# Accumulating the cosine layers' seven-product sums in PSUM, and writing the scales' diagonal one step ahead

## The chip, the cores and the metric

The kernel runs on one core of one Trainium2 chip. The metric is device time in microseconds; the kernel before takes 1402.75 us (median of three runs, 1401.98 to 1403.76). The engines are named as in the profile: PE is the matrix engine (TensorE), PEld its weight loads, DVE is VectorE, ACT is ScalarE, POOL is GpSimd and SP is SyncE, which issues transfers. Each engine carries out its instructions in the order in which they were recorded, and waits where an operand is not there yet.

## The reference

Three stages follow each other. Attention has 2 batches, 8 heads, 768 positions and a head size of 64, with four sink columns and a window of 128. Its output, 1536 tokens by 512, goes to a mixture of 8 ReLU experts whose gate is normalised eight times by rows and columns. The last stage multiplies by the cosine:

```python
for e in range(E):                       # 8 experts, 512 -> 1024 -> 512
    h = np.maximum(x @ w1[e], 0.0)
    out += P[:, e:e+1] * (h @ w2[e])
...
h = x @ w_in                             # 512 -> 2048
g = h * np.cos(h)
return g @ w_out                         # 2048 -> 512
```

All is float32, so the kernel splits each float32 operand, scaled by a power of two, into a high and a low float16 half, and multiplies three times (high by high, high by low, low by high).

## The kernel before

The last stage is cut into two halves of 1024 hidden columns, and so has the shape of two more experts: `e` runs from 0 to 9, where 0 to 7 are ReLU experts and 8 and 9 are cosine experts. Each runs for batch `b` = 0 and then 1 (768 tokens each). The four passes with `e` of 8 and 9 are called the cosine layers C0 to C3 here.

A layer begins with its first multiplication, x by w1. It is done with seven products in place of eight (Winograd's form of Strassen's scheme): tokens are cut into two halves of 384, hidden columns into 4 pairs of blocks, `j` = 0 to 3, of 128 columns. For each `j` the products 0 to 6 are six matmuls of 128x384 each, and four blocks come out: `j` (low) and `NJ + j` (high), each for both halves of the tokens. A product with its surroundings is a step; `tick()` at its end records what other work is due there (loads, splits of the next weights, parts of the cosine). Such work is put on the list with `put(t0, every, steps)`, and `flush()` first runs what is in the list `late`.

In ReLU layers (`g1`, L925) products 0, 4, 3, 6 of a chain pile up in one bank of PSUM ("A"), 5 and 2 in another ("B"), 1 in a third ("C"). Between them ACT copies the sum out (L930), because each partial sum is needed by itself, and DVE adds two of them (L934). In cosine layers (`g1_sums`, L968) each product has a bank of its own, from a ring of five, and the sums are made by DVE: 7 adds per chain (L989) after one copy by ACT (L997).

A block h then goes through `act_cos` (L881): ACT converts it to whole turns (L887), DVE reduces it (L890), ACT takes Sin and Square (L895, L896), DVE multiplies by h (L899), and POOL writes the high half (L901) and the low half (L903) into HH. These parts are recorded one to three steps after each other.

The second multiplication (`g2_mm`, L1021) takes three matmuls of 128x512 per tile of 128 tokens and block of 128 columns: an item. There are 6 tiles and 8 blocks in a layer, so 48 items. In cosine layers the items of three tiles are put beside the products of the first multiplication (the list `fill`): when a chain `j` begins, the items of chain `j - 1` are appended, and one item is recorded after each product (none in the last chain, where six are kept back, `KEEP = 6`). The other three tiles follow whole.

A scale (`scales`, L122) needs the largest of 128 partial maxima, one in each partition. DVE cuts it to a power of two and multiplies the unit matrix by it (L144, the diagonal), PE multiplies a matrix of ones with the diagonal (L145), so that every partition holds all 128 values, and one step later DVE takes the maximum (L149) and its reciprocal. Diagonal and product are recorded in the same step. With several scales at once (attention's values) all diagonals share one tile, so each waits for the product before it.

Of the kernel before, what the change touches and what calls it, by code (L numbers as in the profile page):

```python
# [40 lines left out]
def kernel(  # L41
# [14 lines left out]
    nc = tc.nc  # L56
# [62 lines left out]
    diag = res.tile([128, 128], BF16, name="diag")  # L119
    top_bank = ["l"]  # L120

    def scales(parts, n, clamp, keep, tag, then, squares=False):  # L122
# [36 lines left out]
        late.append(rest)  # L159
# [140 lines left out]
    def attention():  # L300
# [411 lines left out]
        put(10, 1, p0[7:9])  # L712
        put(11, 0.5, p0[9:-1:2])
# [83 lines left out]
    def experts(before):  # L797
# [83 lines left out]
        def act_cos(src, ft, half, sc):  # L881
# [26 lines left out]
        KEEP = 6  # L908
        pend = []

        def settle():
            if pend:
                pend.pop()()
# [11 lines left out]
        def g1(b, j0, chain, act):  # L925
# [42 lines left out]
        def g1_sums(b, j, act, fill, keep):  # L968
            q = {}

            def prod(o, use):

                ps = ring["g1"].next()[:, 0:HT]
                n = 0
                for kk in range(2):
                    for wi, xi in ((0, 0), (0, 1), (1, 0)):
                        nc.tensor.matmul(  # L977
                            ps, W1O[:, j, wi, o, kk, :], XO[b][:, kk, o, xi, :],
                            start=(n == 0), stop=(n == 5))
                        n += 1  # L980
                if len(fill) > keep:
                    fill.popleft()()
                settle()
                pend.append(lambda: use(ps))
                tick()

            def add(tag, x, y):
                t = ring[tag].next()
                nc.vector.tensor_tensor(out=t, in0=x, in1=y, op=ALU.add)  # L989
                return t  # L990

            def out(x, y, ft, half):
                act(add("c", x, y), ft, half)

            def use0(ps):
                q["p0"] = ring["t"].next()
                nc.scalar.activation(out=q["p0"], in_=ps, func=AF.Copy)  # L997

            def use4(ps):
                q["u"] = add("t", ps, q["p0"])  # L1000

            def use5(ps):
                q["u5"] = add("t", ps, q["u"])

            def use3(ps):
                out(ps, q["u5"], NJ + j, 1)
                q["v"] = add("t", ps, q["u"])

            prod(0, use0)
            prod(4, use4)  # L1010
            prod(1, lambda ps: out(ps, q["p0"], j, 0))
            prod(5, use5)
            prod(2, lambda ps: out(ps, q["u5"], NJ + j, 0))
            prod(3, use3)
            prod(6, lambda ps: out(ps, q["v"], j, 1))


        orders = ([0, NJ, 1, NJ + 1, NJ + 2, NJ + 3, 2, 3], [f for j in range(NJ) for f in (j, NJ + j)])
# [13 lines left out]
        def layers(e, b, act, so):  # L1032
# [4 lines left out]
            top_bank[0] = "l" if e < E else "g1"  # L1037
            if e < E:
                for j0 in range(0, NJ, 2):
                    g1(b, j0, CHAIN if e or b else ONE, act)  # L1040
            else:

                for j in range(NJ):
                    if j == 1:
                        ps = {t: ring["g2"].next() for t in range(U3)}
                    for f in (j - 1, NJ + j - 1) if j else ():
                        for t in ps:
                            fill.append(lambda t=t, f=f: g2_mm(e, t, ps[t], [f], False))
                    g1_sums(b, j, act, fill, KEEP if j == NJ - 1 else 0)
# [14 lines left out]
            if e >= E:  # L1064
                for t in ps:
                    fill.append(lambda t=t: g2_mm(e, t, ps[t], order[-2:-1]))
                m = len(fill)
                for k in range(m):
                    fill.popleft()()
                    for _ in range(U3 * (NJ - 1) * k // m, U3 * (NJ - 1) * (k + 1) // m):  # L1070
                        tick()
                late = order[-1:]
            for t in tiles if e < E else range(NT):
                if t in ps:
                    g2_mm(e, t, ps[t], late)
# [72 lines left out]
        for e in range(E + 2):  # L1148
# [3 lines left out]
            if e == E:  # L1152
                banks(g1=(2, 3, 6, 0, 1))
                ring.update(t=Ring(TMP[:, n] for n in range(4)), c=Ring(TMP[:, n] for n in range(4, 9)))
# [88 lines left out]
```

## Time and profile before

| | |
|---|---|
| median of 3 runs | 1402.75 us |
| profiled execution | 1399.94 us, its span 1398.2 us |
| PE busy | 1289.7 us (92%) |
| DVE, ACT, POOL busy | 896.0, 694.1, 641.2 us |
| mean granted clock of PE | 0.964 |
| C0, C1, C2, C3 | 76.08, 61.43, 64.44, 62.21 us |

Times in the trace count from the first instruction. A timeline row gives start, duration, engine, line, operation, tiles, shapes and, in brackets, how long the engine had stood idle and what ended it. The source lines are those of the kernel above; the row of a helper names the helper's line. The last matmul's end of a row is modelled, and a row overlaps with the next.

### The profile page before, as it was taken

Reading aid. Unit: us, or ns where it says so; the run is one execution under the profiler, and the core shown is the slowest. Engines: PE = TensorE matmul, PEld = TensorE weight load, DVE = VectorE, ACT = ScalarE, POOL = GpSimd, SP = SyncE. Lnnn points to the kernel's source line nnn. Section 1 sums busy time; section 2 is a strip of 40 time slices with the busy share of each in tenths; the row PEclk is TensorE's granted clock in tenths of the full one; section 3 lists DMA queues with packets and bytes.
Section 4 is the critical chain, followed back from the end, with each engine's and each line's share of the span. In section 5 each row is a group of like instructions: output and inputs, shape, how many; then the busy total and the mean of one; then the engine's idle time right before and its main releaser. Section 6 shows DMA issues by size and latency. Waiting matters only on the chain.

```text
span 1398.2 us, 19777 instructions
## 1 busy us (share of the span) xinstructions
PE 1289.7 (92%) x7299; PEld 683.2 (49%) x7299; DVE 896.0 (64%) x1853; ACT 694.1 (50%) x1374; POOL 641.2 (46%) x782
## 2 busy tenths in 40 slices
PE   5657899999999999999999999999999987998998
PEld 4533455454554545455454555545455443444444
DVE  8996762865556653855655575484565689678664
ACT  5654664462635346164443616436263647566443
POOL 4555463521524264163336427234442657276534
PEclk7767899999999999999999999999999999999999
DMA  9997663011112310501331050141112232200001
GB/s 233 164 166 175 119 138 101 1 61 61 61 61 73 124 59 7 191 1 60 92 106 61 30 166 1 60 133 64 61 38 81 47 93 54 74 1 0 31 16 45
DMA packets 140689, 108.78 MB, mean 78 GB/s; under 512 B 100144, under 2 KB 115504, under 8 KB 140592
## 3 DMA queue, kind: packets, MB, share of 16 engines
q1 hardware_dynamic: 126512, 77.22, 21.6%
q0 software_dynamic: 7168, 25.17, 5.9%
q10 hardware_dynamic: 6912, 5.13, 1.4%
q8 instruction: 57, 0.93, 0.3%
q14 instruction: 40, 0.33, 0.1%
HBM read 71.84 MB, written 11.53 MB: 60 GB/s over the span
## 4 chain that ended last, share of the span: by engine, by line
PE 58%; ACT 11%; DVE 11%; POOL 5%; issue 2%; DMA 1%; SPq 0%; POOLq 0%; DVEq 0%
PE bank L1026 37%; PE bank L958 18%; ACT tmp L878 4%; ACT hh L877 4%; PE bank L977 3%; DVE tmp L934 2%; DVE tmp L989 2%; ACT tmp L930 2%; DVE wm L162 1%; POOL hh L903 1%; DVE tmp L899 1%; DVE w1o L185 1%; POOL hh L901 1%; DVE xs L185 1%; POOL hh L879 1%
## 5 line engine op out<-in xcount | busy, mean ns | idle before, releaser
L1026 PE MATMUL bank<-w2s,hh 128*128 128x512 f16 x2880 | 641.5, 380 | 19.5 <-POOL hh L901 9.8
L958 PE MATMUL bank<-xo,w1o 128*128 128x384 f16 x2688 | 457.5, 330 | 16.1 <-ACT tmp L930 8.4
L1026 PEld LDWEIGHTS <-hh 128*128 128x128 f16 x2880 | 280.0, 98 | 359.2 <-POOL hh L903 15.1
L879 POOL TENSOR_TENSOR hh<-tmp,hh 128x384 f16<-128x384 f32 x256 | 230.2, 918 | 395.3 <-ACT tmp L878 390.6
L958 PEld LDWEIGHTS <-w1o 128*128 128x128 f16 x2688 | 262.0, 99 | 212.0 <-issue 43.2
L930 ACT ACTIVATE tmp<-bank 128x384 f32<-128x384 f32 x192 | 91.6, 485 | 328.4 <-PE bank L958 328.3
L934 DVE TENSOR_TENSOR tmp<-bank,tmp 128x384 f32<-128x384 f32 x192 | 104.0, 554 | 216.3 <-ACT tmp L930 183.0
L877 ACT ACTIVATE hh<-tmp 128x384 f16<-128x384 f32 x192 | 99.7, 519 | 59.5 <-DVE tmp L934 59.2
L977 PE MATMUL bank<-xo,w1o 128*128 128x384 f16 x672 | 119.3, 328 | 1.9 <-DMA xo<-xs 1.1
L1090 DVE SCALAR_TENSOR_TENSOR acc<-bank,PS,acc 128x512 f32<-128x512 f32 x84 | 62.7, 747 | 74.9 <-PE bank L1026 74.5
L878 ACT ACTIVATE tmp<-tmp 128x384 f32<-128x384 f32 x192 | 100.4, 523 | 6.1
L977 PEld LDWEIGHTS <-w1o 128*128 128x128 f16 x672 | 65.9, 98 | 54.7 <-issue 7.7
L901 POOL TENSOR_SCALAR hh<-tmp 128x384 f16<-128x384 f32 x64 | 44.8, 699 | 102.9 <-DVE tmp L899 102.3
L162 DVE TENSOR_REDUCE wm<-st 128x1 f32<-128x1024 f32 x72 | 86.4, 1209 | 4.0 <-DMA st<-w_in 4.0
L184 ACT ACTIVATE w1o<-S,s 128x1024 f16<-128x1024 f32 x40 | 45.8, 1146 | 78.5 <-POOL S L271 77.9
L185 DVE SCALAR_TENSOR_TENSOR w1o<-st,s,w1o 128x512 f16<-128x512 f32 x72 | 66.1, 951 | 18.1 <-ACT w1o L184 18.1
L185 DVE SCALAR_TENSOR_TENSOR w1o<-S,s,w1o 128x1024 f16<-128x1024 f32 x40 | 55.3, 1382 | 28.9 <-ACT w1o L184 28.9
L989 DVE TENSOR_TENSOR tmp<-bank,tmp 128x384 f32<-128x384 f32 x112 | 59.8, 550 | 20.2 <-PE bank L977 17.6
L903 POOL TENSOR_TENSOR hh<-tmp,hh 128x384 f16<-128x384 f32 x64 | 68.2, 1066 | 5.3
L185 DVE SCALAR_TENSOR_TENSOR w2s<-st,s,w2s 128x512 f16<-128x512 f32 x72 | 57.6, 816 | 19.4 <-ACT w2s L184 19.4
L558 ACT ACTIVATE xo<-xo,nm 128x260 f32<-128x260 f32 (+1 forms) x96 | 41.8, 482 | 30.9 <-DVE nm L544 24.0
L895 ACT ACTIVATE tmp<-tmp,scl 128x384 f32<-128x384 f32 x64 | 39.1, 611 | 34.9 <-DVE tmp L890 34.6
(183 smaller groups left out, 1326.1 us busy)
## 6 DMA issues: line engine op xcount, KB each, us to landing
st<-in_moe_w_dram SPq DMA_DIRECT2D x56, 512.0 KB, 6.0
f<-in_moe_w_in_dram POOLq DMA_DIRECT2D x16, 512.0 KB, 4.5
f<-in_moe_w_out_dram POOLq DMA_DIRECT2D x16, 512.0 KB, 4.2
w2p<-in_moe_w_dram SPq DMA_DIRECT2D x8, 512.0 KB, 4.3
w_in<-x POOLq DMA_DIRECT2D x16, 256.0 KB, 4.4
w_out<-x POOLq DMA_DIRECT2D x16, 256.0 KB, 4.2
st<-w_out SPq DMA_DIRECT2D x8, 512.0 KB, 5.3
st<-w_in SPq DMA_DIRECT2D x8, 512.0 KB, 6.5
```

Source lines behind the costliest of these rows:

```text
L162: nc.vector.tensor_reduce(out=dst, in_=src, axis=axis, op=ALU.max, apply_absolute_value=True)
L185: late.append(lambda: nc.vector.scalar_tensor_tensor(out=lo, in0=src, scalar=s, in1=hi, op0=ALU.mult, op1=ALU.subtract))
L877: nc.scalar.activation(out=hi, in_=src, func=AF.Relu)
L878: nc.scalar.activation(out=dst, in_=src, func=AF.Relu)
L879: nc.gpsimd.tensor_tensor(out=lo, in0=dst, in1=hi, op=ALU.subtract)
L903: nc.gpsimd.tensor_tensor(out=lo, in0=k, in1=hi, op=ALU.subtract)
L930: nc.scalar.activation(out=t, in_=ps, func=AF.Copy)
L934: nc.vector.tensor_tensor(out=t, in0=ps, in1=t, op=ALU.add)
L958: nc.tensor.matmul(ps, W1O[:, j0 + c, wi, o, kk, :], XO[b][:, kk, o, xi, :], start=(n == 0 and o in (0, 5, 1)), stop=(n == 5), skip_group_ ...
L977: nc.tensor.matmul(ps, W1O[:, j, wi, o, kk, :], XO[b][:, kk, o, xi, :], start=(n == 0), stop=(n == 5))
L989: nc.vector.tensor_tensor(out=t, in0=x, in1=y, op=ALU.add)
L1026: nc.tensor.matmul(ps, HH[:, hi, f, t * 128:(t + 1) * 128], w[:, wi, f, :], start=(f == order[0] and n == 0), stop=(f == order[-1] and n = ...
```

## The change

Cosine layers go through `g1` too, all four chains in one call. The order `STAG` puts the second half of chain `j` beside the first half of chain `j + 1`. Chains use the bank pairs in turn (`c % 2`), product 1 always bank "C". `g1_sums` is gone. Product 6's sum is copied out by ACT inside `act_cos` (`dst`). The items of a block are appended seven steps (`WAIT`) after its last product, and three are kept back (`KEEP = 3`); the first three tiles are now 3 to 5, and the order of the blocks is high before low. What drains a product is recorded after the next product as before, or ahead of it where the next one uses the same bank. This replaces the rule that in the first layer of the first expert drained product 3 at once, ahead of the step's other work.

In `scales` the diagonal is written a step before its product, and with several scales each has a tile of its own; a product that would need bank "C" in a cosine layer is put off while product 1 is near (`blocked`).

```diff
-        bank = ring[top_bank[0]].next()
-        held.append(bank)
-        ps = bank[:, 0:n * 128].rearrange("p (n w) -> p n w", w=128)
-        for k in range(n):
-            d = diag
+        ds = [diag] if n == 1 else [W1O[:, NJ - 1, 1, k, 0].bitcast(BF16) for k in range(n)]
+        for k, d in enumerate(ds):
             nc.vector.tensor_scalar(out=d, in0=eye, scalar1=p2[:, k:k + 1], scalar2=None, op0=ALU.mult)
-            nc.tensor.matmul(ps[:, k], one16, d, start=True, stop=True)
-        def rest():
+        def product():
+            if blocked[0]():
+                late.append(product)
+                return
+            bank = ring[top_bank[0]].next()
+            held.append(bank)
+            ps = bank[:, 0:n * 128].rearrange("p (n w) -> p n w", w=128)
+            for k, d in enumerate(ds):
+                nc.tensor.matmul(ps[:, k], one16, d, start=True, stop=True)
+            late.append(lambda: rest(bank, ps))
...
-        late.append(rest)
+        late.append(product)
...
-        put(10, 1, p0[7:9])
-        put(11, 0.5, p0[9:-1:2])
+        put(10, 2, p0[7:9])
+        put(12, 0.5, p0[9:-1:2])
...
             inv2, half_inv, n2pi = sc
+            if dst is not None:
+                nc.scalar.activation(out=dst, in_=src, func=AF.Copy)
+                src = dst
...
-        KEEP = 6
+        KEEP, WAIT = 3, 7
...
-                ps = ring[HOME[o] if HOME[o] == "C" else HOME[o] + str(c)].next()[:, 0:HT]
+                ps = ring[HOME[o] if HOME[o] == "C" else HOME[o] + str(c % 2)].next()[:, 0:HT]
                 q[HOME[o], c] = ps
+                if pend and pend[0][0] == (c, HOME[o]):
+
+                    settle()
...
+                if beside:
+                    beside(k)
                 settle()
-                pend.append(lambda c=c, o=o, ps=ps: use(c, o, ps))
-                if chain is ONE and o == 3:
-                    settle()
+                pend.append(((c, HOME[o]), lambda c=c, o=o, ps=ps: use(c, o, ps)))
                 tick()
...
+        STAG = sorted((2 * k + 7 * j, j, o) for j in range(NJ) for k, o in enumerate((0, 5, 4, 1, 3, 6, 2)))
+        STAG = [(j, o) for _, j, o in STAG]
+
+        def ready(j, o):
+
+            return STAG.index((j, o)) + WAIT
...
+                ps = {t: ring["g2"].next() for t in tiles[:U3]}
+                when = {ready(j, o): f for j in range(NJ - 1) for o, f in ((3, NJ + j), (6, j))}
...
+                def beside(k):
+                    step[0] = k
+                    if k in when:
+                        fill.extend(lambda t=t, f=when[k]: g2_mm(e, t, ps[t], [f], False) for t in ps)
+                    if len(fill) > KEEP:
+                        fill.popleft()()
+
+                blocked[0] = lambda: any(o == 1 for _, o in STAG[step[0]:step[0] + 2])
+                g1(b, 0, STAG, act, beside)
```

On PE, around the scales' product in the first multiplication of the third expert (bank5 receives it, bank3 and bank1 are products of the chains; L145 becomes L153, L958 becomes L973). Before:

```order
L958 LDWEIGHTS w1o_71
L958 MATMUL bank3_81<-xo0_69,w1o_71 128x384
L145 LDWEIGHTS one16_93
L145 MATMUL bank5_83<-diag_94,one16_93 128x128
L958 LDWEIGHTS w1o_71
L958 MATMUL bank1_79<-xo0_69,w1o_71 128x384
```

After:

```order
L973 LDWEIGHTS w1o_71
L973 MATMUL bank1_79<-xo0_69,w1o_71 128x384
L153 LDWEIGHTS one16_93
L153 MATMUL bank5_83<-diag_94,one16_93 128x128
L973 LDWEIGHTS w1o_71
L973 MATMUL bank2_80<-xo0_69,w1o_71 128x384
```

The scales' product has moved behind the whole product in bank1, one step later.

On ACT, the beginning of C1 (L997 and L942 are copies out of a bank, L887 and L899 the conversion, L895 and L907 Sin, L896 and L908 Square). Before:

```order
L997 ACTIVATE tmp_77<-bank2_80 128x384
L887 ACTIVATE tmp_77<-tmp_77,scl_10469 128x384
L895 ACTIVATE tmp_77<-tmp_77,scl_10469 128x384
L896 ACTIVATE tmp_77<-tmp_77 128x384
L887 ACTIVATE tmp_77<-tmp_77,scl_10469 128x384 x2
```

After:

```order
L942 ACTIVATE tmp_77<-bank2_80 128x384 x2
L899 ACTIVATE tmp_77<-tmp_77,scl_10465 128x384
L942 ACTIVATE tmp_77<-bank3_81 128x384
L907 ACTIVATE tmp_77<-tmp_77,scl_10465 128x384
L908 ACTIVATE tmp_77<-tmp_77 128x384
L942 ACTIVATE tmp_77<-bank2_80 128x384
L899 ACTIVATE tmp_77<-tmp_77,scl_10465 128x384
L907 ACTIVATE tmp_77<-tmp_77,scl_10465 128x384
L908 ACTIVATE tmp_77<-tmp_77 128x384
L894 ACTIVATE tmp_77<-bank2_80 128x384
L899 ACTIVATE tmp_77<-tmp_77,scl_10465 128x384
L942 ACTIVATE tmp_77<-bank3_81 128x384
```

Copies out of bank2 and bank3, the "A" banks of chains 0 and 1, now stand between the parts of the cosine; the first chain's copy of product 3 (the third from bank2) comes right behind the first Sin and Square.

## Rows read from the trace of the kernel before

**Rows 1.** First line of the page: the span.

```profile
span 1398.2 us, 19777 instructions
```

**Rows 2.** Busy time by stretch, C0 to C3: each engine's us, clock, DMA.

```profile
1130.03:1206.11 76.08, 63.35 (x316) 30.91 (x314) 63.06 (x123) 45.66 (x84) 40.81 (x50) 0.96 0.35 86
1206.11:1267.54 61.43, 59.36 (x314) 30.07 (x313) 46.85 (x80) 37.68 (x67) 41.36 (x47) 1.00 0.03 13
1267.54:1331.98 64.44, 59.47 (x314) 30.00 (x312) 43.19 (x74) 31.15 (x58) 30.61 (x34) 1.00 0.06 21
1331.98:1394.19 62.21, 59.46 (x313) 29.91 (x311) 39.93 (x71) 27.93 (x52) 27.89 (x32) 1.00 0.07 26
```

**Rows 3.** PE's timeline in C3: start, us, instruction, count, idle before.

```profile
1331.98 7.96 PE L977 MATMUL bank<-xo,w1o 128*128 128x384 f16 x48
...
1342.09 1.14 PE L977 MATMUL bank<-xo,w1o 128*128 128x384 f16 x6
1343.07 0.81 PE L1026 MATMUL bank<-w2s,hh 128*128 128x512 f16 x3
...
1376.97 17.22 PE L1026 MATMUL bank<-w2s,hh 128*128 128x512 f16 x79 [0.37 <-POOL hh L903]
```

**Rows 4.** PE's waits from 1130 to 1398: us in total, times, longest.

```profile
PE bank L1026 <- POOL hh L901: 9.8, 6, 3.8
PE bank L1026 <- POOL hh L903: 7.4, 15, 0.8
PE bank L145 <- DVE diag L144: 3.4, 2, 1.9
PE bank L977 <- DMA xo<-xs: 1.1, 1, 1.1
```

**Rows 5.** PE's timeline in the experts: waits before the scales' product.

```profile
430.69 0.22 PE L145 MATMUL bank<-diag,one 128*128 128x128 bf16 x1 [0.93 <-DVE diag L144]
...
1028.68 0.22 PE L145 MATMUL bank<-diag,one 128*128 128x128 bf16 x1 [0.93 <-DVE diag L144]
1086.62 0.26 PE L145 MATMUL bank<-diag,one 128*128 128x128 bf16 x1 [4.11 <-DVE diag L144]
```

**Rows 6.** Waits in the first 130 us: DVE on the scales' products.

```profile
DVE diag L144 <- PE bank L145: 1.8, 5, 0.4
...
DVE allm L149 <- PE bank L145: 1.4, 4, 0.4
```

**Rows 7.** ACT's timeline in the first expert: a pair of exponentials.

```profile
114.81 0.91 ACT L558 ACTIVATE xo<-xo,nm 128x260 f32<-128x260 f32 x2 [1.50 <-DVE nm L544]
```

**Rows 8.** ACT's timeline in C3.

```profile
1341.16 0.60 ACT L887 ACTIVATE tmp<-tmp,scl 128x384 int32<-128x384 f32 x1
1341.66 0.60 ACT L895 ACTIVATE tmp<-tmp,scl 128x384 f32<-128x384 f32 x1
1342.30 0.52 ACT L896 ACTIVATE tmp<-tmp 128x384 f32<-128x384 f32 x1
1342.73 0.47 ACT L997 ACTIVATE tmp<-bank 128x384 f32<-128x384 f32 x1
1343.10 0.60 ACT L895 ACTIVATE tmp<-tmp,scl 128x384 f32<-128x384 f32 x1
```

**Rows 9.** DVE's timeline in C3: an add and a reduction.

```profile
1336.08 0.56 DVE L989 TENSOR_TENSOR tmp<-bank,tmp 128x384 f32<-128x384 f32 x1 [0.42 <-PE bank L977]
1336.56 0.61 DVE L890 SCALAR_TENSOR_TENSOR tmp<-tmp,scl 128x384 f32<-128x384 int32 x1
```

**Rows 10.** ACT's timeline in C0: the table load and two operand splits.

```profile
1137.42 1.28 ACT L895 ACT_TABLE_LOAD   x1
...
1140.29 0.79 ACT L184 ACTIVATE xs<-acc,s 128x256 f16<-128x256 f32 x2
```

**Rows 11.** Busy time by stretch, after the wait of 4.11 us.

```profile
1086.40:1089.90 3.50, 3.28 (x12) 1.58 (x12) 0.98 (x6) 1.06 (x3) 1.71 (x4) 0.51 0.71 136
```

**Rows 12.** Who waited for the ReLU layers' copies from 200 to 1126 us.

```profile
  PE bank L958: 7.3, 13
```

More of the change, by code (lines that the diff above doesn't have):

```diff
@@ L119 @@
     diag = res.tile([128, 128], BF16, name="diag")
+    blocked = [lambda: False]
     top_bank = ["l"]
@@ L138, in scales, with rest @@
             nc.vector.tensor_scalar(out=i, in0=i, scalar1=0x7F800000, scalar2=None, op0=ALU.bitwise_and)
[L139 to L147 removed]
+        ds = [diag] if n == 1 else [W1O[:, NJ - 1, 1, k, 0].bitcast(BF16) for k in range(n)]
+        for k, d in enumerate(ds):
+            nc.vector.tensor_scalar(out=d, in0=eye, scalar1=p2[:, k:k + 1], scalar2=None, op0=ALU.mult)
+        def product():
[8 more added lines that the diff above has]
+            late.append(lambda: rest(bank, ps))
+        def rest(bank, ps):
             allm = sm.tile([128, n], F32, tag=f"allm{n}", name="allm")
@@ L879, in act_relu, with act_cos @@
             nc.gpsimd.tensor_tensor(out=lo, in0=dst, in1=hi, op=ALU.subtract)
-        def act_cos(src, ft, half, sc):
+        def act_cos(src, ft, half, sc, dst=None):
             inv2, half_inv, n2pi = sc
+            if dst is not None:
+                nc.scalar.activation(out=dst, in_=src, func=AF.Copy)
+                src = dst
             hi, lo = (HH[:, hl, ft, half * HT:(half + 1) * HT] for hl in range(2))
@@ L923, in experts, with g1 @@
         HOME = {0: "A", 4: "A", 3: "A", 6: "A", 5: "B", 2: "B", 1: "C"}
-        def g1(b, j0, chain, act):
+        def g1(b, j0, chain, act, beside=None):
             q = {}
@@ L961, in g1 @@
                         n += 1
+                if beside:
+                    beside(k)
                 settle()
-                pend.append(lambda c=c, o=o, ps=ps: use(c, o, ps))
-                if chain is ONE and o == 3:
-                    settle()
+                pend.append(((c, HOME[o]), lambda c=c, o=o, ps=ps: use(c, o, ps)))
                 tick()
[L968 to L1015, printed above, removed]
@@ L1018, in experts @@
-        orders = ([0, NJ, 1, NJ + 1, NJ + 2, NJ + 3, 2, 3], [f for j in range(NJ) for f in (j, NJ + j)])
+        STAG = sorted((2 * k + 7 * j, j, o) for j in range(NJ) for k, o in enumerate((0, 5, 4, 1, 3, 6, 2)))
+        STAG = [(j, o) for _, j, o in STAG]
+        def ready(j, o):
+            return STAG.index((j, o)) + WAIT
+        orders = ([0, NJ, 1, NJ + 1, NJ + 2, NJ + 3, 2, 3], [f for j in range(NJ) for f in (NJ + j, j)])
         tiles = [*range(U3, NT), *range(U3)]
@@ L1036, in layers @@
             order = orders[e >= E]
-            top_bank[0] = "l" if e < E else "g1"
+            top_bank[0] = "l" if e < E else "C"
             if e < E:
@@ L1041, in layers @@
             else:
[L1043 to L1049, printed above, removed]
+                ps = {t: ring["g2"].next() for t in tiles[:U3]}
+                when = {ready(j, o): f for j in range(NJ - 1) for o, f in ((3, NJ + j), (6, j))}
+                step = [0]
+                def beside(k):
[6 more added lines that the diff above has]
+                g1(b, 0, STAG, act, beside)
+                blocked[0] = lambda: False
+                for f in order[-4:-1]:
+                    if ready(f % NJ, 3 if f >= NJ else 6) >= len(STAG):
+                        fill.extend(lambda t=t, f=f: g2_mm(e, t, ps[t], [f], False) for t in ps)
             settle()
@@ L1064, in layers @@
             if e >= E:
-                for t in ps:
-                    fill.append(lambda t=t: g2_mm(e, t, ps[t], order[-2:-1]))
                 m = len(fill)
@@ L1069, in layers @@
                     fill.popleft()()
-                    for _ in range(U3 * (NJ - 1) * k // m, U3 * (NJ - 1) * (k + 1) // m):
+                    for _ in range(12 * k // m, 12 * (k + 1) // m):
                         tick()
                 late = order[-1:]
-            for t in tiles if e < E else range(NT):
+            for t in tiles:
                 if t in ps:
-                    g2_mm(e, t, ps[t], late)
+                    g2_mm(e, t, ps[t], late, False)
                 else:
@@ L1152, in experts @@
             if e == E:
-                banks(g1=(2, 3, 6, 0, 1))
-                ring.update(t=Ring(TMP[:, n] for n in range(4)), c=Ring(TMP[:, n] for n in range(4, 9)))
+                ring["c"] = Ring(TMP[:, n] for n in range(9))
             if e + 1 < E + 2:
@@ L1198, in experts @@
                     so = k[:, 3:4]
-                    act = lambda src, ft, half, sc=sc: act_cos(src, ft, half, sc)
+                    act = lambda src, ft, half, dst=None, sc=sc: act_cos(src, ft, half, sc, dst)
                 layers(e, b, act, so)
```

4 lines of the change are left out of this document (2 added, 2 removed).

## The prediction

> **What bounds the kernel now.** I read the busy time by stretch first, then TensorE's (PE) timeline and waits in each stretch, then the engine that released each wait. The profiled execution took 1399.94 us, of which the span is 1398.2 [rows 1]; the median of the three timed runs, 1402.75, lies 2.8 above it, and I add the differences found in the trace to that median. From about 200 us on PE is the bound. The four cosine layers, C0 to C3, stand end to end in the last 264 us, and PE is busy for 63.35 of 76.08, 59.36 of 61.43, 59.47 of 64.44 and 59.46 of 62.21 us [rows 2]. The same work fills each: 28 first-layer products and 48 second-layer items of three matmuls. A product takes 0.98 us (its start at 1342.09 to the next row's at 1343.07), an item 3 x 17.22 / 79 = 0.65 us [rows 3]. The floor of a cosine layer is 28 x 0.98 + 48 x 0.654 = 58.8 us. What can be won there is what lies above it: 17.3, 2.6, 5.6 and 3.4 us.
>
> What PE waited for in those layers: 17.2 us for the high and low halves that GpSimd writes (9.8 + 7.4), and 3.4 us for the scales' diagonal [rows 4]. Five banks in rotation make the products themselves wait for almost nothing: the first eight of C3 run in 7.96 us [rows 3].
>
> **The scales' diagonal.** Its product stands in PE's fixed order, so PE stands still until VectorE has written the diagonal. In the ReLU experts this is 0.93 us six times, at the same place of six experts; the first and the last are shown, and one more wait of 4.11 us stands before C0 [rows 5]. The change puts one step, a product of 0.98 us, between the diagonal and its product. The six waits of 0.93 are then covered with 0.05 to spare: 6 x 0.93 = 5.6. Of the 4.11 us one step goes: 1.0. Together 6.6 us. The scale arrives one step later for its splits; the steps that read it stand behind it in the program and are first due after it, so I price this at nothing. If the cover fell (VectorE's queue a step behind), the 5.6 come back: bounds 0 and 9.7 (all of 5.6 and 4.11).
>
> In the attention part PE waits for diagonals too, but VectorE sets the pace there, and it waits on the products only 1.8 + 1.4 us [rows 6]. Bounds: it gains 3.2 us if VectorE alone paces, nothing if not. On the other side, in the first expert the drain of product 3 is no longer recorded before the step's other work; its ScalarE copy can fall behind a pair of exponentials of 0.91 us [rows 7], four times 0.91: 3.6 us lost. I take 2 gained, nearer to the waits that are in the trace.
>
> **The cosine layers.** What goes: 64 VectorE adds (of 112, four of seven per chain) and the waits of rows 4 for GpSimd, since second-layer items now follow their blocks by seven steps and three items are held back. At the end of the first layer's products ten items stand in hand, 6.5 us of PE work, against one block's way (copy, add, convert, reduce, Sin, Square, multiply, two GpSimd passes). What is late next is the bank. Before, a product's bank came free after one read and four others were there. Now products 0, 4, 3, 6 of a chain pile up in one bank, and each may start only when ScalarE has copied the sum before it. The copies per chain rise from one to four (0, 4, 3 and, inside the activation, 6): 48 more copies. Between products 3 and 6 only one other product stands (none in the last chain).
>
> A copy takes 0.47 us, and the row after it starts 0.37 later. A block of the cosine costs ScalarE a conversion (the next row starts 0.50 later), Sin (Square starts 0.64 later) and Square (next row 0.43 later) [rows 8]: 1.57 us. A chain is then 4 x 0.37 + 4 x 1.57 = 7.8 us of ScalarE against 7 x 0.98 = 6.9 us of PE while no items run beside it, as in the first 14 steps. On top come the stretches in which its order holds it: for an add (0.56) and for a reduction (0.61) [rows 9].
>
> I walked ScalarE's order of rows through the first layer with these times, t = 0 at the layer's first product, results readable 0.2 us after a product's nominal end:
> - First block: product 1 of chain 0 ends at 3.90, add 4.10 to 4.66, conversion 4.72 to 5.32, then a copy for chain 1, reduction to 5.99, Sin and Square until the engine is free at 7.09. Behind them stands the copy of chain 0's product 3, done at 7.57. Product 6 could have started at 6.83: it waits 0.8.
> - From 5.22 to 17.27 ScalarE issues five copies (1.9), four conversions (2.0) and five Sin/Square pairs (5.35), 9.2 us, and stands about 2.8 us for adds and reductions. Then comes the copy of chain 1's product 3, done at 17.74. Its product 6 could start at 14.45: it waits 3.35.
> - In chain 2 items lengthen the steps, and the wait is 0.15. In chain 3 products 3 and 6 are neighbours: 1.3.
> Sum 5.6 us, layer 58.8 + 5.6 = 64.4. C1 to C3 become 3 x 64.4 = 193.2 against 61.43 + 64.44 + 62.21 = 188.1: 5.1 us lost.
>
> C0 has more in ScalarE's queue: a table load of 1.28 us and the splits of the other batch's operands (0.79 for two and, of the same operand, a third taken at 0.7), three operands ahead of the long wait [rows 10]: 1.28 + 3 x 1.5 = 5.8. With its first DMA wait (1.1 [rows 4]) and the low clock (0.96 over 76 us, 3.0 [rows 2]) kept, C0 is 58.8 + 5.6 + 5.8 + 1.1 + 3.0 = 74.3, 1.8 less than 76.08. Bounds: 66 (ScalarE's extra work hidden, clock full) and 82 (double the extra queue).
>
> In the trace, PE was granted 0.51 over the 3.5 us after the 4.11 us wait, the lower level of 1.2 GHz [rows 11], while C2, which lost 5.6 us in several shorter waits, ran without such a fall. A wait of 3.35 is shorter than 4.11: nothing taken, 1.75 us a layer (half of 3.5) kept as the upper bound.
>
> Sum: -6.6 - 2.0 - 1.8 + 5.1 = -5.3 us: 1394.6 on the profiled execution, 1397.5 on the median.
>
> **Rivals.**
> - ScalarE keeps up. For it: in the ReLU layers sums already pile up in banks, and PE's waits for the copies are 7.3 us in 13 waits, 0.56 each [rows 12]. Against: a ReLU block has no Sin, Square or reduction. At four waits of 0.56 a layer is 61.0: C1 to C3 183.1 (-5.0), C0 about 68 (-8), with the 8.6 of the diagonal and attention -21.6: about 1381.
> - Slower: ScalarE's queue ahead of the copy of product 3. If rows follow each other by their full durations and not by the shorter starts, the same walk gives waits of 0.95, 4.15, 0.9 and 1.8, 7.8 in all, and a wait of 4.15 is as long as the 4.11 after which the clock fell: 58.8 + 7.8 + 1.75 = 68.3. C1 to C3 lose 16.8, C0 0.4, and 8.6 are won: +8.6, 1411. It decides from 6.9 us of waits a layer (5.6 + 5.3 / 4). For it: starts that overlap are shown only for independent neighbours. Against: the neighbours in rows 8 are just that.
> - No change: the diagonal's wait only passes to the next bank's copy, and of the first term nothing is left: +1.3, 1404.
>
> The Trainium skill speaks for the second of these: "Perfetto Trace Analysis", section Optimizing Tensor Performance, asks that independent groups of matmuls rotate through different banks, so that the draining of one overlaps the matmuls of the next. The trace agrees for the kernel before (7.96 us for eight products, no wait [rows 3]); by that rule alone every chain would wait for its drains, as in that rival. The page "TensorE: Matmul & The Clock Gate", section A second HAM failure mode, adds that many short idles between groups can drop the clock; the one fall in rows 11 follows a long wait, not short ones, and the sum goes without it.
>
> **How the numbers follow.** Forecast 0.46, ScalarE keeps up 0.20, slower 0.21, no change 0.13. The forecast's own range is 1391 to 1404 (attention -3 to +3, C0 and the walk by 2 each). A measurement of this kernel can tell 0.2%, 2.8 us, from no change. The forecast is beyond it four times in five, the rest mostly within: faster 0.36 + 0.20 = 0.56; same 0.07 + 0.13 = 0.20; slower the rest, 0.24. The range of eight in ten leaves out the far ends of both outer rivals: 1384 to 1409.
>
> **What would show it.** Right: no wait before the scales' product in the experts; no wait on GpSimd's halves in C0 to C3; in their place waits of the products on ScalarE's copies, the longest of each layer in its second chain, some 3 us; C1 to C3 each near 64 us; VectorE's adds down by 64 and copies up by 48. Wrong: C1 to C3 at 60 to 61 us (ScalarE in time), a granted clock below 0.97 there (the slower rival), or waits of 0.9 us on another engine where the diagonal's were.

## The result, and the profile after

The changed kernel takes 1414.82 us (median of four runs, 1412.1 to 1415.72) against 1402.37 (four runs, 1400.93 to 1403.76) of the kernel before: ratio 1.0086, 95% interval 1.0068 to 1.0103. It is 12.45 us slower; 5.3 us faster was forecast. The profiled execution took 1414.56 us; it is 14.6 above the profiled one of before, 2 more than the medians are apart.

First the page after: its span, which answers to [rows 1], the busy times, and the group of the copies in the seven-product chains (line, engine, operation, count | busy us, mean ns | idle before, and what ended most of it).

```profile
span 1412.9 us, 19703 instructions
...
PE 1292.8 (91%) x7299; PEld 684.9 (48%) x7299; DVE 863.4 (61%) x1789; ACT 714.2 (51%) x1422; POOL 639.6 (45%) x782
...
L942 ACT ACTIVATE tmp<-bank 128x384 f32<-128x384 f32 x240 | 114.5, 483 | 346.9 <-PE bank L973 345.8
```

ACT has 240 copies on this line (192 from the ReLU layers and 48 from the cosine layers) and is busy only half of the span. As an average it looks free; the share says nothing of where its queue is late.

Busy time by stretch, C0 to C3 after, in the columns of [rows 2]:

```profile
1117.10:1199.64 82.54, 65.24 (x315) 32.02 (x314) 59.25 (x107) 50.97 (x96) 39.74 (x50) 0.92 0.34 79
1199.64:1275.14 75.50, 63.79 (x315) 31.69 (x313) 44.42 (x72) 45.28 (x82) 44.08 (x48) 0.93 0.03 11
1275.14:1341.69 66.55, 60.42 (x313) 30.93 (x312) 29.62 (x49) 33.93 (x65) 27.95 (x32) 0.97 0.06 21
1341.69:1408.90 67.21, 60.87 (x313) 30.86 (x311) 30.93 (x56) 33.24 (x64) 27.99 (x32) 0.97 0.06 24
```

C0 begins 12.9 us earlier than before (1117.10 against 1130.03), and then the four layers give back 27.6: they last 291.80 us in place of 264.16. The waits are the length less the busy time:

| layer | length before, after | PE busy before, after | waits before, after |
|---|---|---|---|
| C0 | 76.08, 82.54 | 63.35, 65.24 | 12.7, 17.3 |
| C1 | 61.43, 75.50 | 59.36, 63.79 | 2.1, 11.7 |
| C2 | 64.44, 66.55 | 59.47, 60.42 | 5.0, 6.1 |
| C3 | 62.21, 67.21 | 59.46, 60.87 | 2.8, 6.3 |

Of the 27.6 us, 19.0 are more waiting and 8.7 are the same matmuls taking longer, which is the clock (the granted clock fell from 0.96, 1.00, 1.00, 1.00 to 0.92, 0.93, 0.97, 0.97).

PE's waits over the same part, 1100 to 1413 us, answer to [rows 4] (us in all, times, longest):

```profile
PE bank L973 <- ACT tmp L942: 33.7, 17, 5.3
PE bank L1000 <- ACT acc L1076: 4.5, 1, 4.5
PE bank L973 <- DMA xo<-xs: 1.1, 1, 1.1
PE bank L1000 <- POOL hh L915: 0.9, 2, 0.4
...
```

GpSimd's 17.2 us have become 0.9. In their place PE waits 33.7 us for ACT's copies out of the bank that the next product of the same chain wants. PE's timeline in C3, which answers to [rows 3], shows all four of the layer's waits:

```profile
1349.41 6.99 PE L973 MATMUL bank<-xo,w1o 128*128 128x384 f16 x42 [0.73 <-ACT tmp L942]
1359.87 1.14 PE L973 MATMUL bank<-xo,w1o 128*128 128x384 f16 x6 [3.48 <-ACT tmp L942]
1360.84 1.41 PE L1000 MATMUL bank<-w2s,hh 128*128 128x512 f16 x3
1362.04 2.13 PE L973 MATMUL bank<-xo,w1o 128*128 128x384 f16 x6
...
1372.22 1.14 PE L973 MATMUL bank<-xo,w1o 128*128 128x384 f16 x6 [0.44 <-ACT tmp L942]
...
1381.45 1.14 PE L973 MATMUL bank<-xo,w1o 128*128 128x384 f16 x6 [1.61 <-ACT tmp L942]
```

The third row is an item that takes 1.20 us to the next row's start and the fourth a product of 1.92, where at the full clock they take 0.65 and 0.98. ACT's timeline ahead of the long wait, in the manner of [rows 8]:

```profile
1357.49 0.52 ACT L908 ACTIVATE tmp<-tmp 128x384 f32<-128x384 f32 x1
1357.92 0.47 ACT L942 ACTIVATE tmp<-bank 128x384 f32<-128x384 f32 x1
1358.29 0.60 ACT L907 ACTIVATE tmp<-tmp,scl 128x384 f32<-128x384 f32 x1
1358.92 0.52 ACT L908 ACTIVATE tmp<-tmp 128x384 f32<-128x384 f32 x1
1359.35 0.47 ACT L942 ACTIVATE tmp<-bank 128x384 f32<-128x384 f32 x1
```

The copy that PE needs is the last row, behind two Sines and Squares; PE goes on at 1359.87, as this copy ends. The clock after such waits, by stretch, in C2 (behind a wait of 3.41 us), in C3 (behind 3.48), and in C1 (behind 4.23 and behind 4.46), answers to [rows 11]:

```profile
1292.70:1296.10 3.40, 2.90 (x9) 1.31 (x9) 2.27 (x4) 1.68 (x4) 1.73 (x2) 0.51 0.00 0
1360.90:1364.30 3.40, 3.40 (x11) 1.40 (x10) 1.78 (x3) 2.24 (x5) 3.17 (x4) 0.50 0.01 2
1217.60:1224.40 6.80, 5.31 (x16) 2.31 (x16) 3.30 (x8) 3.79 (x9) 3.49 (x4) 0.50 0.00 0
1258.50:1261.90 3.40, 3.40 (x10) 1.21 (x8) 2.41 (x4) 3.40 (x6) 3.32 (x4) 0.50 0.02 5
```

PE is granted 0.50, the lower level of 1.2 GHz, for 3.4 us (once 6.8), where an item and a product take about twice as long as at the full clock. By this, half of the time that PE is busy in such a stretch is lost, an estimate from these rows: 1.5 us in C2, 1.7 in C3, and 4.4 in C1 (half of 5.31 and 3.40).

C1 has one wait that no other layer has. PE and then ACT there:

```profile
1251.78 1.67 PE L1000 MATMUL bank<-w2s,hh 128*128 128x512 f16 x7
1257.92 17.39 PE L1000 MATMUL bank<-w2s,hh 128*128 128x512 f16 x72 [4.46 <-ACT acc L1076]
```

```profile
1249.08 1.10 ACT L193 ACTIVATE w1o<-st,s 128x512 f16<-128x512 f32 x2
1256.14 1.15 ACT L193 ACTIVATE w1o<-S,s 128x1024 f16<-128x1024 f32 x1 [5.96 <-POOL S L280]
1257.20 1.82 ACT L1076 ACTIVATE acc<-bank,scl 128x512 f32<-128x512 f32 x3
```

The three tiles of the second multiplication are done and must be copied out (L1076) before their banks can take the next three. The copy is ready to go, but in ACT's order a split of the next weights (L193) stands ahead of it, and this waits 5.96 us for GpSimd. The change put the steps that such splits belong to (12 of them) all beside the ten held items. Before, nine stood there, and one behind each of the first three tiles. These lines of the change do it:

```diff
+                    for _ in range(12 * k // m, 12 * (k + 1) // m):
+                        tick()
...
-                    g2_mm(e, t, ps[t], late)
+                    g2_mm(e, t, ps[t], late, False)
```

### The profile page after: what moved, and what is told of

Read it like the earlier page. It is cut to its first block, busy times and chain, and to the rows that moved or that the text cites. A ratio compares the mean times of both kernels' runs of the same rounds, so it can differ in the third digit from the quotient of the medians.

```text
span 1412.9 us, 19703 instructions
## 1 busy us (share of the span) xinstructions
PE 1292.8 (91%) x7299; PEld 684.9 (48%) x7299; DVE 863.4 (61%) x1789; ACT 714.2 (51%) x1422; POOL 639.6 (45%) x782
## 4 chain that ended last, share of the span: by engine, by line
PE 61%; ACT 13%; DVE 9%; POOL 3%; issue 2%; DMA 0%; POOLq 0%; ACTq 0%; DVEq 0%
PE bank L1000 38%; PE bank L973 22%; ACT tmp L887 4%; ACT hh L886 4%; DVE tmp L946 3%; ACT tmp L942 2%; DVE tmp L902 1%; ACT tmp L907 1%; ACT tmp L908 1%; DVE xs L194 1%; DVE wm L171 1%; DVE tmp L911 1%; POOL hh L888 1%; DVE w1o L194 1%; ACT tmp L899 0%
## 5 line engine op out<-in xcount | busy, mean ns | idle before, releaser
L973 PE MATMUL bank<-xo,w1o 128*128 128x384 f16 x3360 | 583.4, 331 | 57.4 <-ACT tmp L942 49.6
L973 PEld LDWEIGHTS <-w1o 128*128 128x128 f16 x3360 | 329.6, 99 | 296.8 <-issue 85.6
L942 ACT ACTIVATE tmp<-bank 128x384 f32<-128x384 f32 x240 | 114.5, 483 | 346.9 <-PE bank L973 345.8
L946 DVE TENSOR_TENSOR tmp<-bank,tmp 128x384 f32<-128x384 f32 x240 | 129.8, 554 | 245.5 <-ACT tmp L942 198.0
L887 ACT ACTIVATE tmp<-tmp 128x384 f32<-128x384 f32 x192 | 100.4, 523 | 6.1
L193 ACT ACTIVATE w1o<-S,s 128x1024 f16<-128x1024 f32 x40 | 45.8, 1146 | 78.9 <-POOL S L280 78.2
L193 ACT ACTIVATE w2s<-st,s 128x512 f16<-128x512 f32 x72 | 46.0, 708 | 22.5 <-DVE s L164 22.5
L583 POOL TENSOR_TENSOR parts<-xo,parts 128x512 f16<-128x512 f32 (+1 forms) x38 | 41.0, 1083 | 33.4 <-ACT parts L578 31.2
L907 ACT ACTIVATE tmp<-tmp,scl 128x384 f32<-128x384 f32 x64 | 39.1, 611 | 28.0 <-DVE tmp L902 27.9
L902 DVE SCALAR_TENSOR_TENSOR tmp<-tmp,scl 128x384 f32<-128x384 int32 x64 | 47.1, 744 | 7.9 <-ACT tmp L899 7.9
```

Source lines behind the costliest of these rows:

```text
L193: nc.scalar.activation(out=hi, in_=src, func=AF.Copy, scale=s)
L887: nc.scalar.activation(out=dst, in_=src, func=AF.Relu)
L942: nc.scalar.activation(out=t, in_=ps, func=AF.Copy)
L946: nc.vector.tensor_tensor(out=t, in0=ps, in1=t, op=ALU.add)
L973: nc.tensor.matmul(ps, W1O[:, j0 + c, wi, o, kk, :], XO[b][:, kk, o, xi, :], start=(n == 0 and o in (0, 5, 1)), stop=(n == 5), skip_group_ ...
```

## Experiments

Theory: in the cosine layers the bank "A" of each chain is now read three times in the middle of the chain, by copies that stand in ACT's fixed order behind the cosine's own work; PE stands idle for them, and where it stands long the clock falls too. Rivals: the scales' diagonal or the later drain took the time; GpSimd's or DVE's part of a block holds PE, and not ACT's queue; or the clock falls by itself. Differences are of medians. Those from the kernel before are beside its runs on the same chip; those between two changed kernels leave out that the medians of the kernel before differ by up to 1.4 us from chip to chip (1401.0 to 1402.4).

**x1_diag and x2_cos: the two halves of the change.** x1 is the kernel before with the scales' part alone, x2 the change with the scales and the drain of the ReLU experts as before.

```diff
 x1, on the kernel before: scales() of the change, its put(10, 2, ...), put(12, ...), and
-                    t1, t2 = (T0 + -5, T0 + 10, 6, ...
+                    t1, t2 = (T0 + -5, T0 + 10, 5, ...
 x2, on the change:
+        if not cosine[0]:
+            ...        # diagonal and product in one step, as before
+                if chain is ONE and o == 3:
+                    settle()
```

> The kernel before, with the scales' part of the change alone (diagonal a step ahead, a tile for each, the moved steps of attention, the first expert's maxima 5 steps apart); cosine layers and the early drain of product 3 as before. Theory A: the 12.9 us by which C0 began earlier come from the diagonal alone, and the loss lies in the cosine layers alone. Then C0 begins near 1117 us, the six waits of 0.93 are gone, and the time is 1402.4 - 12.9 - 1 to 3 (the diagonal's waits in C0), 1387 to 1390. Theory B: about half of it (the 6.4 us before the second batch of the first expert) comes from the later drain of product 3 there. Then C0 begins near 1121 and the time is 1392 to 1396.

> The changed kernel with the scales before the cosine layers, and the drain of product 3 in the first expert, as before the change: the cosine part alone. Theory A: C0 to C3 take what they take in the changed kernel, 82.5, 75.5, 66.6 and 67.0, so the time is 1402.4 + 27 = 1429 (1426 to 1432). Rival: the two parts hinder each other in the cosine layers (the later scale); then they are shorter here and the time is 1418 to 1424.

x1 took 1391.93 us, 0.9923 of before (0.9905 to 0.9941), 9.1 us less, and C0 begins at 1121.50: 8.5 us earlier, so the scales do not explain all of the 12.9. x2 took 1429.3 us, 1.0198 (1.018 to 1.0216), 28.3 us more; its C0 begins at 1130.81 and its waits are those of the change:

```profile
PE bank L997 <- ACT tmp L966: 33.7, 17, 5.3
PE bank L1026 <- ACT acc L1102: 4.5, 1, 4.5
```

The loss is in the cosine layers alone, and what goes before them changes nothing in it. (x2 holds all of the cosine part, the steps moved in C1 too.)

**x5_drain and x6_diag_drain: the rest of the early gain.** x5 is the kernel before with only the later drain of product 3 in the first expert's first layer; x6 is x1 and x5 together.

```diff
+                if chain is ONE and o == 6:
+                    settle()
                 n = 0
...
-                if chain is ONE and o == 3:
-                    settle()
```

> The kernel before with one rule of the change alone: in the first layer of the first expert product 3 is drained after the step's other work, just ahead of product 6. x1_diag began C0 near 1121.5 us in its trace, the changed kernel at 1117.1 and two kernels like it at 1114.5. Theory B: the 4.4 to 7 us between them are this rule, since ScalarE and VectorE do the attention's work while product 3 runs, in place of standing for its end. Then the time is 4 to 7 us below that of before, 1394 to 1397. Rival, as the prediction had it: the copy falls behind the exponentials, and nothing or up to 3.6 us is lost, 1401 to 1405; the difference would then be how the attention happened to run.

> The kernel before with all of the change but the cosine layers: the diagonal a step ahead and the later drain of product 3. If the two add up: 1401 - 9 (x1_diag) - 4 to 7 = 1385 to 1388. Rival: both fill the same gaps of the attention part; then no better than x1_diag, 1391 to 1392.

x5 took 1397.43 us (ten runs), 0.9973 (0.9956 to 0.999), 4.3 less; C0 begins at 1125.49, 4.5 earlier. Of the two rows, the first is the kernel before and the second x5, over the first expert's first batch:

```profile
111.36:222.32 110.96, 96.58 (x776) 52.65 (x777) 68.16 (x209) 62.68 (x130) 61.57 (x70) 0.90 0.66 136
```

```profile
111.63:217.93 106.30, 91.23 (x775) 50.03 (x776) 67.44 (x209) 62.16 (x130) 60.97 (x70) 0.93 0.66 142
```

PE's busy time for the same matmuls falls by 5.35 us, more than the stretch itself (4.66): the gain is the clock (0.90 to 0.93), not less waiting. x6 took 1386.16 us, 0.9884 (0.9859 to 0.991), 15.6 less, and C0 begins at 1114.76. The parts add up: -15.6 here and +28.3 in x2 are +12.7, and the whole change measures +12.45.

**x3_nosquare: is it ACT's queue?** The change with ACT's Square left out, so the output is another function.

```diff
                 nc.scalar.activation(out=k, in_=k, func=AF.Sin, scale=half_inv)
-                nc.scalar.activation(out=k, in_=k, func=AF.Square, scale=SQRT2)
```

> The changed kernel with ScalarE's Square left out of the cosine (the output is then another function). Theory A: PE waits for ScalarE's queue, so with 0.43 us less a block the wait before product 6 of the second chain falls from 3.4 us to below 1.5, the half clock after it goes in C2 and C3, and these fall from 66.9 to 61 to 63 us; total 1397 to 1403. Rival: the wait is the way of one copy through the bank (drain, add, next product) and hardly depends on the other work of ScalarE: it stays above 2.5 us, total 1410 to 1415.

It took 1395.08 us, 0.9952 (0.9937 to 0.9966), 19.7 less than the change and below the range that was expected. PE's waits from C2 to the end fall from 12.4 us in 8 to 5.0 in 5, longest 1.4 (here the lines read L972 and L941):

```profile
PE bank L972 <- ACT tmp L941: 5.0, 5, 1.4
```

Work taken from ACT alone shortens PE's wait for a copy that nobody touched, so PE waits for ACT's queue; GpSimd and DVE kept all of their work. Whether the amount of work in that queue counts or the place of the copy in it, this run can't tell; x8 does. The eviction wait in C1 stays at 4.45: the split ahead of it waits for GpSimd. In C0 the waits for copies hardly change either (2.00, 6.08, 1.39 and 3.89 us, in the change 2.56, 5.34, 1.95 and 4.16): what holds them there is not the Square.

**x4_ticks: C1's eviction.** The change with the tail's steps recorded as before.

```diff
-                    for _ in range(12 * k // m, 12 * (k + 1) // m):
+                    for _ in range(9 * k // m, 9 * (k + 1) // m):
                         tick()
...
                     g2_mm(e, t, ps[t], late, False)
+                    if e >= E:
+                        tick()
```

> The changed kernel with the steps behind the products spread as before: nine beside the ten held items, and one behind each of the first three tiles, in place of twelve beside the items. Theory A: PE's wait of 4.46 us for an eviction in C1 comes from these three steps, since they put splits of the next weights ahead of the first eviction in ScalarE's queue, and a split waits for GpSimd. Then that wait and the half clock after it go, C1 falls from 75.5 to about 69.5 and the total by 5 to 7, to 1408 to 1410. Rival: the eviction waits because the first three tiles are now 3 to 5 or because GpSimd is late whatever the steps; then C1 stays above 74.

It took 1408.69 us, 1.0051 (1.0036 to 1.0066), 6.1 less than the change. C1 runs from 1196.59 to 1265.86, 69.3 us in place of 75.5; the wait of 4.46 and the low clock behind it are gone, and a wait of 1.31 for a copy is new at the start of C2.

**x7_dummy: does the clock fall because PE stands idle?** x4 with 18 matmuls more in each cosine layer, whose result nobody reads, in an unused bank, ahead of the product that waits longest.

```diff
+                if beside and (c, o) == (1, 6):
+                    for _ in range(18):
+                        nc.tensor.matmul(BANK[4][:, 0:HT], W1O[:, 0, 0, 0, 0, :], XO[b][:, 0, 0, 0, :], start=True, stop=True)
```

> x4_ticks with 18 further matmuls of 128x384 (18 x 0.163 = 2.9 us, into a bank not yet in use, their result dropped) ahead of product 6 of the second chain in each cosine layer, where PE waits 3.4 to 5.3 us. Theory A: the half clock after this wait follows from PE standing idle. Then the waits shrink to 0.5 to 2.4 us, the clock stays at 1.00 behind them, each layer ends 1.7 us earlier and the total is 3 to 7 us below x4_ticks, 1402 to 1406. Rival: the clock falls whatever PE does there, or the added matmuls delay the products: 1408 to 1412.

It took 1402.99 us (ten runs), 1.0008 (0.9995 to 1.0022): with more work, 5.7 less than x4. PE's timeline in C2 of x7; the 18 fill what was a wait, of which 0.48 is left:

```profile
1279.89 3.09 PE L973 MATMUL bank<-xo,w1o 128*128 128x384 f16 x18
1283.46 1.14 PE L977 MATMUL bank<-xo,w1o 128*128 128x384 f16 x6 [0.48 <-ACT tmp L943]
```

Busy time by stretch, the first row of x7 from just before C1 (it begins at 1196.28) to its end, then of x4 behind its two long waits in C2 and C3:

```profile
1195.00:1400.00 205.00, 187.77 (x998) 97.31 (x996) 107.07 (x178) 111.94 (x211) 100.30 (x112) 1.00 0.06 22
```

```profile
1286.40:1289.80 3.40, 3.40 (x11) 1.44 (x10) 1.79 (x3) 2.24 (x5) 3.15 (x4) 0.50 0.00 0
1351.20:1358.00 6.80, 5.67 (x17) 2.45 (x17) 3.48 (x6) 4.15 (x9) 4.34 (x5) 0.50 0.00 1
```

The falls of the clock go with the idle time: where the 18 matmuls fill it, the clock stays at 1.00. In the traces all of the gain lies in C1 to C3, which with the end of the kernel take 209.8 us in x4 and 203.7 in x7. In C0 the same 18 matmuls leave a wait of 2.42, the matmuls behind it are still slow (1.69 for six), and the layer takes 82.2 in both.

**x8_copy5: copy the other operand.** x4, but ACT copies product 5 early, and DVE adds it to the sum of product 3 straight out of PSUM. The read that PE waits for is then DVE's.

```diff
-                elif o == 3:
+                elif o == 5 and beside:
                     copy(c, "w", ps)
-                    out(c, "w", q["B", c], 1, True)
+                elif o == 3:
+                    if not beside:
+                        copy(c, "w", ps)
+                    out(c, "w", ps if beside else q["B", c], 1, True)
```

> x4_ticks, but in the cosine layers ScalarE copies product 5 when it is done, and VectorE adds it to the sum of product 3 straight from PSUM; so product 6 waits for one VectorE add and not for a copy at the end of ScalarE's queue. The same number of copies and adds. Theory A (the place of this one copy in ScalarE's queue makes the long wait): by the same walk the waits of a layer are 0, 1.5, 0 and 0.8, no fall of the clock, C2 and C3 61 to 62.5 us, total 1384 to 1392. Rival (ScalarE's load as such): the wait moves to another copy, C2 and C3 stay above 65, total above 1402.

It took 1385.17 us, 0.9878 (0.9847 to 0.991), 23.5 less than x4. C0 to C3, and PE's waits from C2 on:

```profile
1118.90:1196.06 77.16, 63.36 (x315) 31.14 (x314) 59.23 (x107) 50.49 (x96) 39.80 (x50) 0.96 0.36 85
1196.06:1259.34 63.28, 60.43 (x314) 31.08 (x313) 43.68 (x65) 43.60 (x80) 42.80 (x48) 0.97 0.03 12
1259.34:1321.84 62.50, 58.87 (x314) 30.51 (x312) 34.32 (x57) 34.76 (x67) 28.33 (x33) 1.00 0.06 22
1321.84:1382.94 61.10, 58.71 (x313) 30.43 (x311) 32.80 (x55) 32.69 (x64) 27.36 (x32) 1.00 0.07 27
```

```profile
PE bank L976 <- DVE tmp L946: 4.7, 4, 1.2
PE bank L976 <- ACT tmp L942: 1.4, 1, 1.4
```

ACT makes as many copies as before this edit. Only one of them moved, to the sum of product 5, and no product is seen to wait for that one: the wait of 1.4 that is left on a copy stands at the beginning of C2, ahead of product 4. So it is the place of the copy in ACT's order that PE waited for, and not ACT's load. C2 and C3 keep the full clock with waits of 1.1 to 1.4 us and are shorter than before the change by 1.9 and 1.1; C0 and C1 are longer by 1.1 and 1.9. Accumulating in one bank, so mended, gains nothing over the four layers, and the 16.6 us by which x8 is below the kernel before are what x6 has without it (15.6).

**x9_xlate and x10_all: the rest of C0, two misses.** C0 of x8 still holds one wait of 5.54. x9 has x8's operand splits for the second batch later and closer together, x10 also the maxima of the next w2.

```diff
-                put(HT_ + 5 if b else HT_ + 4, 4.5 if b else 7.0, xops)
+                put(HT_ + 17 if b else HT_ + 4, 3.5 if b else 7.0, xops)
 x10, on x9:
-                    t2, t1 = (0, 5, 3.0, 39, 1.25), ...
+                    t2, t1 = (0, 17, 3.0, 39, 1.25), ...
```

> x8_copy5, with the other batch's operand splits begun 17 steps into C0 in place of 5, and 3.5 steps apart in place of 4.5. In x8_copy5 PE still waits 5.54 and 2.91 us in C0 for VectorE adds. Theory A: C0's extra loss comes from these splits in ScalarE's and VectorE's queues ahead of the chains. Then the wait of 5.54 falls to about 1.5 and the half clock behind it goes; about as much work comes into the later steps, so C0 falls by 3 to 7 us, total 1378 to 1383. Rival: the load only moves to the later chains, whose waits grow by as much, or the operands come late for C1: 1384 to 1390.

> x9_xlate, and the maxima of the next expert's second weights, four VectorE reductions of 1.2 us each, begun 17 steps into C0 in place of 5. Theory A: in the early steps of C0 the adds that free a bank stand behind these reductions in VectorE's queue too; 1 to 3 us less than x9_xlate, 1376 to 1381. Rival: they now stand among the operand splits, VectorE's queue is full there, and it is 0 to 4 us more than x9_xlate.

x9 took 1391.01 us, 0.9927 (0.9913 to 0.9942); x10 1393.09, 0.9938 (0.9922 to 0.9955): 5.8 and 7.9 more than x8. PE's timeline in C0 of x9:

```profile
1134.90 1.14 PE L976 MATMUL bank<-xo,w1o 128*128 128x384 f16 x6 [2.09 <-DVE tmp L946]
...
1161.99 2.08 PE L976 MATMUL bank<-xo,w1o 128*128 128x384 f16 x6 [5.07 <-DVE tmp L946]
...
1182.75 1.86 PE L1003 MATMUL bank<-w2s,hh 128*128 128x512 f16 x4 [5.50 <-ACT acc L1081]
```

The wait of 5.54 became 2.09, and two of 5.07 and 5.50 came further on (in x10 6.20 and 5.64): the wait moved from one place to two others. So it is not shown that the splits alone make these waits.

**x11_mixed: each layer by its better form.** x8 with C0 and C1 computed as before the change (`g1_sums`, its order and its rings), C2 and C3 as in x8.

```diff
+            elif e == E:
+                for j in range(NJ):
+                    ...
+                    g1_sums(b, j, act, fill, 6 if j == NJ - 1 else 0)
             else:
```

> x8_copy5 for the second cosine expert (C2, C3), and the cosine layers of the kernel before for the first (C0, C1), where ScalarE and VectorE also split the next operands and weights; the scales and the drain as in the change. Theory A (accumulating pays only where those queues are free): C0 and C1 as in x6_diag_drain, about 76 and 61.5, C2 and C3 as in x8_copy5, 62.5 and 61.1: about 3 us below x6_diag_drain, 1381 to 1385. Rival: what is saved in C2 and C3 is within the spread from run to run, 1385 to 1389.

It took 1383.97 us (five runs), 0.9872 (0.9853 to 0.9891). The intervals of x6, x8 and x11 overlap, so their order is open; all three beat both kernels, by 15 to 18 us and by 28 to 31.

## Why the prediction was wrong, step by step

The two spans are 14.7 us apart where -5.3 was forecast, 20.0 more: 16.1 of it in C1 to C3, 8.3 in C0, and -4.3 before them.

**C1 to C3, "+5.1": measured +21.2 (14.1, 2.1 and 5.0). This is the step that failed.** The walk of ACT's order gave waits of 0.8, 3.35, 0.15 and 1.3; C3 has 0.73, 3.48, 0.44 and 1.61, 6.3 in place of 5.6, each at its place. What failed is what was made of it, in two ways.
- "Nothing taken" for the clock. Behind the wait of 3.48, PE ran 3.4 us at half clock. The waits of 6.3 and 1.7 on the floor of 58.8 are 66.8; the layer took 67.2. C2 likewise: 58.8 + 6.1 + 1.5 = 66.4, measured 66.55. The sentence kept 1.75 a layer as an upper bound, and in C3 the bound was the value. x7 shows that the idle time brings the fall. The reason given, that 3.35 is shorter than the 4.11 behind which the clock fell, left out two falls that C0 of the kernel before has as well. One stands behind two waits of 1.83 and 0.78, with two matmuls between them, and one behind 3.80 (busy time by stretch, as in [rows 2]):

```profile
1145.30:1147.00 1.70, 1.70 (x7) 0.79 (x6) 1.70 (x3) 1.26 (x3) 0.00 (x0) 0.50 0.00 0
...
1185.40:1188.90 3.50, 3.41 (x9) 1.24 (x10) 2.65 (x5) 2.78 (x5) 1.75 (x3) 0.52 0.01 2
```

- C1 was priced as a copy of C3. It also has the weights' maxima and splits of the next expert in the queues (that these lengthen its waits is read from the order; no run takes them out): its long wait is 4.23, followed by 6.8 us at half clock, and the eviction adds 4.46 and another fall. 58.8 + 11.7 of waits + 4.4 of clock = 74.9, measured 75.50. The eviction wait was in no term and no rival; the edit that brought it (12 steps beside ten items) is part of the change but was not priced, and x4 gets 6 us back by undoing it.

**C0, "-1.8": measured +6.5.** 82.54 us is just above the upper bound of 82. The queue's extra work was added as a single delay of 5.8; in the trace it meets PE in four waits (2.56, 5.34, 1.95 and 4.16, sum 14.0). Three of them:

```profile
1128.28 8.67 PE L973 MATMUL bank<-xo,w1o 128*128 128x384 f16 x42 [2.56 <-ACT tmp L942]
...
1142.29 2.08 PE L973 MATMUL bank<-xo,w1o 128*128 128x384 f16 x6 [5.34 <-ACT tmp L942]
...
1169.52 1.86 PE L973 MATMUL bank<-xo,w1o 128*128 128x384 f16 x6 [4.16 <-ACT tmp L942]
```

Behind each the matmuls are slow: 42 take 8.67 us where C3 has 6.99, six take 2.08 and 1.86 where C3 has 1.14. The clock of C0 is 0.92 where the sum kept the 0.96 of before. What makes these waits stays open in part: without the Square they hardly change (x3), and in x9 and x10 later places for parts of the other load only moved them.

**The diagonal, "-6.6": measured -6.4. Attention with the first expert, "-2.0": measured -6.5.** The second batch of the first expert begins 6.5 us earlier (at 215.78), C0 12.9, so 6.4 are won between them. The six waits of 0.93 are gone as forecast: no wait ahead of the scales' product is left between 200 and 1117 us. The wait of 4.11 shrank by 0.65 where 1.0 was forecast; it passed to a copy, and the clock fell behind it as in [rows 11]:

```profile
1073.57 1.50 PE L973 MATMUL bank<-xo,w1o 128*128 128x384 f16 x6 [3.46 <-ACT tmp L942]
```

```profile
1074.20:1077.60 3.40, 3.40 (x14) 1.70 (x12) 1.42 (x6) 1.65 (x5) 1.52 (x3) 0.50 1.22 122
```

Of the 6.5 before the second batch, the scales give 2.0 (it begins at 220.31 in x1 and at 222.32 before) and the later drain the rest. The drain was priced at a loss of up to 3.6; x5 shows a gain of 4.3 (1.4 to 6.2 by its interval), outside the bounds of that term, and it comes by the clock, which the term did not hold. That 8.6 is also near what x1 gives (9.1) is luck: the 2.0 was taken for scales and drain together.

**Rivals.** The slower one had the right sign and mechanism and its 68.3 is near C2 and C3 (66.6 and 67.2), but by too long waits (7.8 a layer; measured 6.1 and 6.3); it too missed C1, C0 and the drain. What tells it from the forecast is the clock alone, by its own words "a granted clock below 0.97" in C1 to C3: C1 is at 0.93, C2 and C3 read 0.97, at the line itself. "ScalarE keeps up" is refuted by waits of 33.7 us. "No change" fails with x1, though the one wait of 4.11 did what it said.

The page "Perfetto Trace Analysis" of the Trainium skill, section Optimizing Tensor Performance, asks that independent groups rotate through different banks. The runs agree only in part. The cosine part, which gives up the rotation within a chain, costs 28.3 us (x2); but x8 gives it up as well, and its C2 and C3 are shorter than before. What cost in C2 and C3 was the place of the copies in ACT's order. The page "TensorE: Matmul & The Clock Gate" of the Trainium skill, section A second HAM failure mode, has the clock oscillate by frequent micro-idles between groups. Here the falls in C1 to C3 stand behind single waits of 3.41 to 4.46 us, and waits of up to 1.4 in C2 and C3 of x8 brought none; the fall in C0 of before, behind 1.83 and 0.78, is nearer to what that section tells.

## What to carry to other kernels

A partial sum that is read in the middle of a chain in one bank turns each read into a wait of the matrix engine on the reader's fixed order: walk that order for each layer with all that other stages have put there, and look for an operand that can be copied at a time when nobody waits. Look for every fall of the clock in the trace before, and not only the one behind the longest wait. Where the walk gives waits like those ahead of the falls, put the half clock into the sum, and keep the sum without it as the other end. An edit that moves where other work is recorded, here three steps, deserves its own term: follow what is queued behind each moved instruction, the evictions too.

## What the runs showed of the hardware

- Matmuls that nobody needs can shorten a kernel: 72 more (18 in each of the four layers) saved 5.7 us (x7 against x4). Those in C1 to C3 filled time in which PE stood idle and kept it at its full clock; the 18 in C0 saved nothing.
- Waits of nearly one size go either way. In the change 3.41 was followed by 3.4 us at 0.51. In x11 C2 has a wait of 3.38 near its beginning and the clock stayed (timeline, then busy time by stretch):

```profile
1258.99 3.25 PE L976 MATMUL bank<-xo,w1o 128*128 128x384 f16 x19 [3.38 <-ACT tmp L942]
```

```profile
1259.00:1262.40 3.40, 3.40 (x21) 2.04 (x21) 0.90 (x5) 1.41 (x4) 0.00 (x0) 1.00 0.00 0
```

  Shorter waits do so too. In x8 the six matmuls behind a wait of 2.20 in C1 take 1.83 us in place of 1.14, while behind one of 2.91 in C0 they take 1.14:

```profile
1212.08 1.83 PE L976 MATMUL bank<-xo,w1o 128*128 128x384 f16 x6 [2.20 <-DVE tmp L946]
```

  What decides between the two is not settled here, and so an estimate of the clock's price needs both ends.
- Independent neighbours on ACT do overlap, as [rows 8] had it: in C3 after, the copy of 0.47 us at 1357.92 has its neighbour start 0.37 later, while the Square at 1358.92 starts 0.63 after the Sin whose result it takes.
